# A four-layer mixer on one core: another fixed order of the same operations, and block 1's tiles turned by DMA

## The chip, the cores and the metric

The kernel runs on one core of a Trainium2 chip. Such a core has five engines that run side by side, each through its own list of instructions in order: TensorE (PE in the profile; its weight loads are PEld), VectorE (DVE), ScalarE (ACT), GpSimd (POOL) and SyncE (SP), which here only issues DMAs. The metric is the device time of one execution in microseconds (us), the median of several runs. Before the change it is 1176.29 us, the median of three runs from 1173.52 to 1176.73.

## The reference

The input x has 2048 positions of 512 features. Two kinds of layer alternate, A, B, A, B, each added to x, and both A layers share their weights, as do both B layers. LN is a layer norm without gain.

```python
# A: sliding attention, 32 heads of 16, 8 keys at distances 0, 2, .., 14 behind
q, k, v = LN(x) @ wqkv
attn = softmax(q . k[pos - 2*j] / 4, over j)
x = x + (sum_j attn_j * v[pos - 2*j]) @ wo
# B, on y = LN(x):
h  = gelu(LN(y) @ w1)                 # four groups of 128 features,
hs = [h0 by +1, h1 by -1, h2 by +2, h3 by -2 positions] @ w2
y1 = y + hs
x  = x + y1 + gelu(LN(y1) @ w3) @ w4  # w3: 512 x 1792
```

## The kernel before

**Numbers.** Most products must keep nearly f32 accuracy with f16 matmuls. Each operand is a high f16 part and a low f16 part (the rest), and three matmuls (high-high, high-low, low-high, the list HLS) stand for one product. A product with 512 inner features and 512 columns is so a group of 12 matmuls.

**Tiling.** The 2048 positions are four blocks of 512, a block is four tiles of 128 rows. With two layers of each kind there are eight block stages, n = 0 to 7: n = 0 to 3 are the blocks of the first A and B layer, n = 4 to 7 those of the second. Per stage there are five parts:
- `p1_stream(n)`: normalises each tile, turns it (features onto the partitions), multiplies by wqkv (three groups a tile) and stores q, k, v to memory (`kvq_d`). The turned tile lies in one of two places `xt`. Stage 0 does this in f32 out of `p1_quarters`.
- `p2(n)`: attention in four units of eight heads: loads `q` and `kv`, products and sums on VectorE, exponentials on ScalarE; the result is turned into `oT`.
- `p3(n)`: the o-projection (12 matmuls a tile with wo), adds x, normalises (`sq_dev`, `power`, `normed`), turns the normalised tile `f` into the place `nT`, and then w1 (four groups of 12 on the whole block) with its gelu into `h`.
- `p4(n)`: w2 on shifted columns of `h` (a group of 12 a tile), normalises and turns again.
- `p5(n)`: 14 chunks of the MLP, each an up group (12 matmuls with w3) and the down-projections (with w4, 3 matmuls a tile) into `acc`. Stage 0 has three tiles here and stage 7 five, since a block's last tile needs the next block's first rows.

**Turning a tile.** There are two ways. `turn_split` does it on TensorE: four transposes of 128x128 f32 by `ident` into PSUM (`mm`), ScalarE's copy of the high part, then either VectorE's subtraction for the low part or, with `minus=True`, a matmul with `minus_id` that subtracts the high part inside PSUM and a second copy by ScalarE. `turn_dma` makes high and low parts before the turn and turns both with one transposing DMA that SyncE issues:

```python
act(key, lambda: A.activation(hv(0), n.t, AF.Copy, scale=sc), ...)   # or VectorE
op(key, [(DVE, lambda: V.tensor_sub(hv(1), n.t, hv(0)), None),
         (POOL, lambda: G.tensor_sub(hv(1), n.t, hv(0)), None)], ...)
op(key, [(SP, lambda: Y.dma_start_transpose(out(), hl.t), None)], ...)
```

The tuple `BY_DMA` names, for the four places where tiles are turned (p1, p3, p4 and p2 in this order), the stages that use `turn_dma`; `MINUS` names those whose `turn_split` uses `minus_id`.

**The order.** The parts only record operations with what they read and write, and with the engines that can do each (`alts`). Nothing is decided at run time: `ORDER` is one list of numbers, 4 x operation + choice of engine, and the instructions are issued in that order, each engine keeping its own. `SLOTS` gives, for every buffer that is used for a while (`mm`, `acc`, `f32`, `g`, `w` and so on), the number of the place that it takes. `KEEP` puts so many filler matmuls ahead of an operation of TensorE: they multiply `ones` by itself (128x256) into a PSUM place that is about to be used. Another 38 (`WARM`) stand at the very start. Since an engine can't overtake within its list, an operation that waits holds everything behind it on that engine.

All operations are issued through one helper, so every instruction of the profile has line L307, and tile names tell them apart.

Of the kernel before, what the change touches and what calls it, by code (L numbers as in the profile page):

```python
# [219 lines left out]
124030101225127334105621120410122314206121117530134025203121225221116035301  # L220
"""

KEEP = {32: 26, 21: 8, 59: 12, 43: 12, 1040: 5, 1048: 16, 1062: 14}


class Buf:
# [67 lines left out]
def tile_mixer(ctx, tc, x_d, wqkv_d, wo_d, w1_d, w2_d, w3_d, w4_d, out_d):  # L294
# [351 lines left out]
    BY_DMA = (4, 5, 6, 7), (2, 3, 4, 5, 6, 7), (1, 2, 3, 4, 5, 6, 7), (2, 3, 4, 5, 6, 7)  # L646
# [712 lines left out]
```

## Time and profile before

| What | us |
|---|---|
| median of three runs | 1176.29 |
| the profiled execution's span | 1172.6 |
| TensorE busy in it | 1155.8 |
| VectorE busy | 895.6 |
| ScalarE busy | 630.4 |
| GpSimd busy | 453.3 |

The profiled execution has no time of its own beside its span: 1172.6 us from its first instruction to its last, 3.7 below the median of the runs. The granted TensorE clock is 1.000 of full speed in the mean over it. Busy times are the time in which at least one instruction of an engine is running; matmuls follow each other in a pipeline, so the time that one holds the engine is the difference of two starts and not its duration. DMA queues move 206.86 MB in all, and the 16 DMA engines are busy for some 61% of the span.

### The profile page before, as it was taken

To read this page: it belongs to the slowest core of one execution; us is meant where nothing else is said; L and a number is where in the kernel's file an instruction comes from. 1 tells how busy PE (TensorE), PEld (TensorE's weight loads), DVE (VectorE), ACT (ScalarE), POOL (GpSimd) and SP (SyncE) were. 2 spreads that over 40 slices of the span, in tenths; PEclk is the share of its full clock that TensorE was granted. 3 is DMA by queue.
4 is the path that set the end of the run, shared out by engine and by line. 5 is a ranking of instruction groups with operands and counts; after the bars stand their busy time and mean duration, and the time that the engine had idled before them with its cause. 6 is when DMAs were issued, how large, how long until landed. Compare 5 with 4: busy or idle time off the path is not lost.

```text
span 1172.6 us, 16187 instructions
## 1 busy us (share of the span) xinstructions
PE 1155.8 (99%) x5760; PEld 568.2 (48%) x5760; DVE 895.6 (76%) x1049; ACT 630.4 (54%) x1221; POOL 453.3 (39%) x441
## 2 busy tenths in 40 slices
PE   9999999899999999999999999999999999999998
PEld 7545555555444444444444444444444444444554
DVE  6888996999998996299976989999936999325112
ACT  5977667556656565464653446564534554444232
POOL 2746347226365455233432363632523272203000
PEclk9999999999999999999999999999999999999999
DMA  7687997365675646784567668873468366425221
GB/s 256 221 275 229 262 308 228 120 214 167 197 193 180 171 108 146 203 226 144 118 186 230 203 170 224 225 196 110 93 186 248 129 172 196 103 69 135 82 75 61
DMA packets 235161, 206.86 MB, mean 176 GB/s; under 512 B 107276, under 2 KB 160772, under 8 KB 235080
## 3 DMA queue, kind: packets, MB, share of 16 engines
q1 hardware_dynamic: 232796, 203.92, 60.5%
q10 hardware_dynamic: 2284, 1.91, 0.5%
q8 instruction: 45, 0.74, 0.3%
q14 instruction: 36, 0.29, 0.1%
HBM read 141.03 MB, written 39.47 MB: 154 GB/s over the span
## 4 chain that ended last, share of the span: by engine, by line
PE 79%; DMA 5%; DVE 4%; ACT 3%; issue 2%; POOL 1%; SPq 0%; ACTq 0%; POOLq 0%; DVEq 0%
PE mm L307 56%; PE acc L307 24%; DMA kvq_d<-ev 3%; DVE L L307 1%; DVE prod L307 1%; DMA xt<-g 1%; ACT junk L307 1%; DMA w<-in_B_w_dram 1%; DMA w<-in_A_x_dram 1%; ACT ev L307 0%; ACT f L307 0%; DVE f L307 0%; POOL g L307 0%; POOL f L307 0%; POOL a L307 0%
## 5 line engine op out<-in xcount | busy, mean ns | idle before, releaser
L307 POOL TENSOR_TENSOR g<-f,g 128x512 f16<-128x512 f32 (+1 forms) x122 | 187.9, 1550 | 315.9 <-ACT g L307 209.5
L307 PE MATMUL acc<-w,g 128*128 128x512 f16 x1302 | 298.3, 379 | 0.0
L307 PE MATMUL mm<-nT,w 128*128 128x512 f16 (+1 forms) x1344 | 292.7, 372 | 0.0
L307 ACT ACTIVATE mm<-mm,s_w 128x512 f32<-128x512 f32 (+2 forms) x158 | 98.4, 624 | 276.6 <-PE mm L307 275.8
L307 PEld LDWEIGHTS <-w 128*128 128x128 f16 x1512 | 141.7, 98 | 152.2
L307 PEld LDWEIGHTS <-g 128*128 128x128 f16 x1398 | 136.6, 98 | 157.6 <-issue 0.9
L307 PE MATMUL mm<-wq_hl,xt 128*128 128x512 f16 x864 | 194.0, 379 | 2.6 <-DMA xt<-g 1.5
L307 PEld LDWEIGHTS <-xt 128*128 128x128 f16 x1008 | 98.3, 98 | 120.1 <-DMA xt<-g 3.8
L307 DVE TENSOR_TENSOR prod<-kv,L 128x2048 f32<-128x2048 f32 (+1 forms) x44 | 146.7, 3336 | 0.1
L307 DVE TENSOR_REDUCE L<-prod 128x128 f32<-128x2048 f32 (+1 forms) x44 | 142.8, 3246 | 0.1
L307 DVE TENSOR_TENSOR prod<-kv,q 128x4096 f32<-128x4096 f32 (+1 forms) x38 | 132.3, 3482 | 7.9 <-DMA kv<-kvq_d 5.0
L307 DVE SCALAR_TENSOR_TENSOR g<-mm,c_g,g 128x512 f16<-128x512 f32 (+1 forms) x53 | 39.2, 740 | 89.8 <-ACT g L307 88.0
L307 DVE TENSOR_TENSOR prod<-prod 128x1024 f32<-128x1024 f32 (+2 forms) x56 | 89.7, 1605 | 0.1
L307 PE MATMUL mm<-nT,w_hl 128*128 128x512 f16 x384 | 87.4, 379 | 0.8 <-ACT nT L307 0.7
L307 PE MATMUL mm<-wo_hl,oT 128*128 128x512 f16 x384 | 86.5, 379 | 0.0
L307 PE MATMUL mm<-w_hl,h 128*128 128x512 f16 x384 | 85.7, 379 | 0.0
L307 ACT ACTIVATE g<-mm,c_g 128x512 f16<-128x512 f32 (+1 forms) x112 | 75.1, 672 | 1.9
L307 PEld LDWEIGHTS <-oT 128*128 128x128 f16 x426 | 41.5, 98 | 48.7 <-issue 0.2
L307 ACT ACT_TABLE_LOAD x42 | 53.9, 1283 | 11.5 <-DVE a L307 7.2
L307 PEld LDWEIGHTS <-w_hl 128*128 128x128 f16 x384 | 37.5, 98 | 45.8 <-issue 1.3
L307 PEld LDWEIGHTS <-h 128*128 128x128 f16 x384 | 37.5, 98 | 45.3 <-DVE h L307 0.4
L307 POOL COPY h<-h 128x2 f16<-128x2 f16 (+1 forms) x20 | 19.3, 982 | 76.2 <-DVE h L307 71.9
(227 smaller groups left out, 1361.7 us busy)
## 6 DMA issues: line engine op xcount, KB each, us to landing
w<-w SPq DMA_DIRECT2D x224, 256.0 KB, 2.7
kv<-kvq_d SPq DMA_DIRECT2D x62, 768.0 KB, 5.3
kvq_d<-ev SPq DMA_DIRECT2D x84, 256.0 KB, 3.0
w<-in_B_w_dram SPq DMA_DIRECT2D x28, 256.0 KB, 4.7
w<-g SPq DMA_DIRECT2D x28, 256.0 KB, 4.2
q<-kvq_d SPq DMA_DIRECT2D x28, 256.0 KB, 5.2
w<-in_A_x_dram SPq DMA_DIRECT2D x16, 256.0 KB, 6.0
x<-in_A_x_dram SPq DMA_DIRECT2D x16, 256.0 KB, 4.0
```

What stands on the lines that cost most here:

```text
L307: i = f(*a, **k).ins
```

## The change

Three lists and one tuple change. `BY_DMA` gets stage 1 in its second entry, so that the four tiles of `p3(1)` go through `turn_dma` rather than `turn_split` with `minus_id`. That replaces four operations a tile (transposes, copy, minus_id matmul, copy) by three (copy, subtraction, DMA); there are 3500 operations after, 3504 before. Each turned tile now takes a place `g` rather than a place `mm`. `ORDER` lists the operations in another order and with other engines for many of those that have a choice: the normalisations, the small operations of `power`, the copies out of PSUM, the two steps of `turn_dma`. `SLOTS` gives other places. `KEEP` goes from seven entries with 93 fillers to three with 70. The first TensorE tile of the list is now tile 0 rather than tile 1 of block 0, and the loads of its four x tiles stand at the head of SyncE's list.

```diff
 ORDER = [int(k) for k in """
-32 1756 20 16 12 8 24 1772 44 40 52 4 56 421 0 104 28 110 118 112 412 60 36 122 417 64 124 68 688 74 128 78 82 428 133
...
 SLOTS = """
-1002301101111010000011212230333200310100102012201301413021612123450331220120011400124255672325063144542571330132544327
...
+103200101000101030301022223111030021012110101201026450033450200126021100012010301000302710300414213503021001241322140
...
-KEEP = {32: 26, 21: 8, 59: 12, 43: 12, 1040: 5, 1048: 16, 1062: 14}
+KEEP = {21: 26, 32: 18, 1048: 26}
...
-    BY_DMA = (4, 5, 6, 7), (2, 3, 4, 5, 6, 7), (1, 2, 3, 4, 5, 6, 7), (2, 3, 4, 5, 6, 7)
+    BY_DMA = (4, 5, 6, 7), (1, 2, 3, 4, 5, 6, 7), (1, 2, 3, 4, 5, 6, 7), (2, 3, 4, 5, 6, 7)
```

In KEEP, 21, 32 and 43 are the turns of block 0's tiles 0, 1 and 2 at the start, 59 the first projection, 1040 the first w2 group of `p4(0)`, and 1048 and 1062 the first two turns behind it.

Read off the two lists, TensorE's order around block 1 is this. Before: the o-projections of block 1 lie among block 0's up and down groups, its four turns and minus_id matmuls among the last down-projections, and the last minus_id matmul stands directly ahead of the four w1 groups; then QKV of tile 1 of stage 4, with w2 of stage 1 between its groups, then of tiles 0 and 2. After: the last o-projection of block 1 is followed by three up and six down groups of block 0, then by the four w1 groups; then the three QKV groups of tile 1 of stage 4, four w2 groups, and QKV of tiles 2 and 0.

More of the change, by code (lines that the diff above doesn't have):

```diff
@@ L44 @@
 ORDER = [int(k) for k in """
[159 rows of a table removed]
[159 rows of a table added]
 """.split()]
 SLOTS = """
-1002301101111010000011212230333200310100102012201301413021612123450331220120011400124255672325063144542571330132544327
-4131031234405741343241130107521302413244265034115325017042333411454601512460012102130211133021201001331010020103103115
-1201302100210313000331302011110312100100033100210201111001300110033120112001111120050001111021330101130001100031330201
-1021100111001312011011011420211011101150120011110115101110211040211201100320311110321003102110033011611201013301020021
@@ L210 @@
-1003301042120101110114305783310103230113302123200041301001313231060505034374214132246031442044353571034022635122126042
-4330516351326130500203042233310213220043550142113471461032022352004410643725402141612217210542331326320145642017311450
-2311404203011314012001214201120311000011101011130110202010013100031210103301030002101110114175042561233213045102121044
-1025321114230410330122033060475163142023113061554115370561360201554331710136344051300002130430002151111000050600300002
-1011110115010210031100610011011101032102010330113328160510130153215210203143013540232514640613201235456017433432020630
@@ L215 @@
-5410526345513661031730210304431520014311400300041601100050101011051631003111210113100120010103110030101010331002300201
-1110114135070400042016353110135303040153206115253603210622371054221335206104520367502510035404303316222174353121255033
-1110041630212050630212110231313102110113101031020103101061001011331012212210011100204281043120031415630032534313226123
-0032402423210625241317322005246130123265435113324721203137314063102531516035224032031621601200115203345215601124323301
-2011557006214514160703223014510276043112256030216216122434172748122105515615510010211001333014153250320033512521300600
@@ L220 @@
-124030101225127334105621120410122314206121117530134025203121225221116035301
+103200101000101030301022223111030021012110101201026450033450200126021100012010301000302710300414213503021001241322140
+233132102103435120312002103451301332200125130112330020461210220011335671720600110011020111101101210010013122001001021
+310030010011201001001101102000100112101200000130011001000011101210000031210101110011300001012000000000111200111101210
+100000200000001401010110001001002101000010210111100000330100020012010011010001120110011031200020100001060101011000110
@@ new lines @@
+100201000010121010111001113760820000122403011002000100123123020007012311056221140302000036010740205100022106302147031
+150602300007140541321101105011112011201101032422153002042060123301017121200425415037060041037602120505411136030021207
+400016161240000111100110211001011000000010110000101001010201200110001101021010110115310201100010226057011112300411400
+102002201241402231034016012351203000711202403561000321710404625310606212150330204570004101000110200001001411101100002
+002120001010000100012001110011310210100001002102011100111313481301000010001113201051101252231004632120123603017040320
@@ new lines @@
+156064701032236100170325201241053004126221700251022020311022100200113000203101110100010100001050120011100112102101110
+011131000100001052206501400130360012030300200223211231044000601237101430121121502367360310407100411172151150262132350
+402000420130002100100000111110110000300001100101000010001200111101141021011000103210001011011131347111102212400521020
+035413106221010417025012310116210301327402121525006641103211700211433560023201041607028612200210041100010200120310442
+551123600101232110542230040760524000010365011430517100250103100670241010241350111102012104012010023141141055224630000
@@ L221 @@
+50310301230720110632101424115735106426117411102313104010101521113612107210120511234130116
 """
-KEEP = {32: 26, 21: 8, 59: 12, 43: 12, 1040: 5, 1048: 16, 1062: 14}
+KEEP = {21: 26, 32: 18, 1048: 26}
 class Buf:
```

317 rows, old and new, of the table ORDER are left out of this document.

## The prediction

> **What bounds the kernel now.** I read the head of the page first, for the engines' shares and the granted clock.
>
> ```profile
> span 1172.6 us, 16187 instructions
> PE 1155.8 (99%) x5760; PEld 568.2 (48%) x5760; DVE 895.6 (76%) x1049; ACT 630.4 (54%) x1221; POOL 453.3 (39%) x441
> PEclk9999999999999999999999999999999999999999
> ```
>
> TensorE is busy for 1155.8 of 1172.6 us at the full clock; no other engine is above 76%. Next, the busy time by stage, to see where the missing 16.8 us lie (columns: length, then busy us of PE, PEld, DVE, ACT, POOL).
>
> ```profile
> 0.00:50.00 50.00, 47.93 (x274) 34.88 (x275) 37.39 (x75) 35.22 (x87) 21.17 (x39) 1.00 0.69 224
> 200.00:250.00 50.00, 46.30 (x287) 28.92 (x286) 48.00 (x49) 29.92 (x60) 11.71 (x13) 1.00 0.46 156
> 340.00:440.00 100.00, 99.06 (x460) 44.75 (x459) 93.49 (x84) 58.64 (x95) 51.66 (x35) 1.00 0.60 162
> 540.00:640.00 100.00, 100.00 (x465) 45.31 (x464) 77.33 (x83) 48.22 (x92) 35.22 (x35) 1.00 0.61 170
> 1140.00:1173.00 33.00, 28.52 (x168) 14.21 (x166) 7.13 (x12) 6.70 (x14) 0.00 (x0) 1.00 0.18 63
> ```
>
> The stretch around 200 to 250 lacks 3.7 us, the first 50 us lack 2.1, 340 to 440 lacks 0.9, and the middle lacks nothing. The last row lacks 4.5, of which 0.4 lies beyond the end: there TensorE is done and only the last additions and stores remain. So about 12 us of idle time can be fought over; otherwise the end is the sum of TensorE's instructions, and VectorE is the one neighbour that is nearly as full (93 of 100 us) where attention runs. TensorE's own waits:
>
> ```profile
> PE mm L307 <- ACT nT L307: 2.6, 4, 1.0
> PE mm L307 <- DMA xt<-g: 1.5, 2, 0.9
> ```
>
> Each is at most 1 us. A change pays here only by taking instructions off TensorE or by closing such a wait, and costs only by opening one.
>
> **The change, part by part.** First the turns of block 1 behind the first attention. For each of four tiles TensorE now does four transposes and a matmul with minus_id, between down-projections (acc).
>
> ```profile
> 300.12 2.11 PE L307 MATMUL acc<-w,g 128*128 128x512 f16 x9
> 302.06 0.38 PE L307 MATMUL mm<-nT,minus_id 128*128 128x512 f16 x1
> 302.28 0.60 PE L307 MATMUL mm<-ident,f 128*128 128x128 f32 x4
> 302.71 2.11 PE L307 MATMUL acc<-w,g 128*128 128x512 f16 x9
> 304.65 0.38 PE L307 MATMUL mm<-nT,minus_id 128*128 128x512 f16 x1
> 305.72 10.52 PE L307 MATMUL mm<-nT,w_hl 128*128 128x512 f16 x48 [0.69 <-ACT nT L307]
> ```
>
> Durations overlap in the pipeline, so I take differences of starts: four transposes hold TensorE 0.43 us (302.28 to 302.71), the minus_id matmul 0.22 (302.06 to 302.28), nine matmuls 1.94 (300.12 to 302.06), so one is 0.216. Neither turned piece waits there, so all of it is on the path: 4 x 0.65 = **-2.6 us**. The wait of 0.69 before w1 (305.72) is for ScalarE's copy of the last turned tile; it goes too, but another arrival takes its place (below), so I count it nowhere.
>
> Second, the filler matmuls (on `ones`, for nothing but to keep TensorE running): KEEP falls from 93 in seven places to 70 in three; the 38 at the start stay.
>
> ```profile
> 1.04 9.83 PE L307 MATMUL mm<-ones 128*128 128x256 f16 x64 [1.04 <-DVE ones L307]
> 221.39 1.91 PE L307 MATMUL mm<-ones 128*128 128x256 f16 x16
> 221.84 0.77 POOL L307 TENSOR_SCALAR f<-f,c,c 128x512 f32<-128x512 f32 x1
> 223.14 0.60 PE L307 MATMUL mm<-ident,f 128*128 128x128 f32 x4
> ```
>
> One filler is (223.14 - 221.39) / 16 = 0.109 us, so 23 fewer are 2.5 us. But the fillers stand in for a wait: the tile that they precede is ready at 221.84 + 0.77 = 222.61 and TensorE takes it at 223.14, 0.53 late. If the waits stay, dropping four of the seven runs gives about 4 x 0.45 (a little under that 0.53, for the handover) = 1.8; if real work fills them, 2.5; if the waits grow, 0. I take **-1.8**, bounds 0 and -2.5. The new order does put more work there: in block 0's mixing, one run of 26 fillers, then three turns in a row, where the old order has 5, 16 and 14 in three places.
>
> Third, one wait that the order itself makes.
>
> ```profile
> 339.31 1.40 SPq L307 DMA_TRANSPOSE xt<-g  x1
> 343.25 4.06 PE L307 MATMUL mm<-wq_hl,xt 128*128 128x512 f16 x18 [0.94 <-DMA xt<-g]
> ```
>
> The second layer's QKV of block 0 takes tiles 1, 0, 2 through two xt places, and the old order finishes tile 1's last QKV group just two groups before tile 2's first. In the new order tile 1's three groups come together, then four w2 groups (4 x 12 x 0.216 = 10.4 us), then the next tile: its place is free long before. **-0.9**, bounds 0 and -0.9.
>
> Fourth, what arrives too late now. Tile 1 of that QKV comes right behind w1, and its input hangs on block 0's last down-projection, which starts at 302.71 above.
>
> ```profile
> 311.93 1.26 SPq L307 DMA_TRANSPOSE xt<-g  x1
> 316.23 0.76 PEld L307 LDWEIGHTS <-xt 128*128 128x128 f16 x5 [0.49 <-DMA xt<-g]
> 316.24 1.04 PE L307 MATMUL mm<-wq_hl,xt 128*128 128x512 f16 x4
> ```
>
> The weight load waits for the landing and gets it just in time: 13.5 us from the start of that down-projection. In the old order 1.94 + 0.22 (and the 0.69 of waiting and its handover) stand ahead of the 48 matmuls of w1; in the new one w1 follows at once, so TensorE comes after 1.94 + 10.37 = 12.3 us. The same chain is then late by **+1.2**, bounds 0 (VectorE gets to it sooner) and +3 (a further 1.8 us if an attention product stands ahead of it on VectorE).
>
> Fifth, the turned tiles themselves. Each now takes a scaled copy (ScalarE or VectorE), a subtraction (VectorE three times, GpSimd once) and one transposing DMA on SP. Block 7 already does this; its last tile is the quick case:
>
> ```profile
> 1015.23 2.75 PE L307 MATMUL mm<-wo_hl,oT 128*128 128x512 f16 x12
> 1018.02 0.75 DVE L307 SCALAR_TENSOR_TENSOR x<-mm,s_wo,x 128x512 f32<-128x512 f32 x1 [0.68 <-PE mm L307]
> 1024.28 1.23 SPq L307 DMA_TRANSPOSE nT<-g  x1
> nT<-g SPq DMA_TRANSPOSE x52, 4.2
> ```
>
> From the end of the o-projection (about 1017.8) to issue is 6.5 us and to landing 4.2 more (the median of the last row), 10.7 in all. The new order has nine block 0 groups of 1.94 us (9 x 0.216 for a down-projection, the same for a three-tile up) between block 1's last o-projection and its w1: 17.5 us. So 0 is taken; the upper bound comes with the rivals. SP gets eight DMAs more: these four, two kv shifts of the start and two stores of the end, both from ScalarE's queue; behind each stand the weight and kv loads.
>
> ```profile
> SPq L307 <- PE mm L307: 219.7, 99, 9.2
> ```
>
> SP spends 219.7 us waiting for TensorE to free places, so 4 x 1.23 us of issuing is covered; without that cover it would be 4.9 us on the loads. The shifts come while TensorE still has its first projections. Both end stores are issued while TensorE still runs (bounds 0 and +0.5).
>
> Sixth, places and engines. Counted over the two lists, TensorE goes from 541 to 533 operations, ScalarE 1028 to 1006, VectorE 894 to 880, GpSimd 390 to 422, SP 651 to 659. Off TensorE these cost nothing in themselves: TensorE's work is what hides them. Attention keeps its distance: between the last QKV group and the first o-projection of block 7 lie 111.5 us of TensorE work in both orders, and 114.1 for block 5.
>
> Sum: -2.6 - 1.8 - 0.9 + 1.2 = -4.1 us on the profiled execution, 1172.6 to 1168.5. That execution's span lies 3.7 below the median 1176.29; I carry the 3.7 over: **1172.2 us**.
>
> **The rivals.** Where two results of this kernel differ by under 0.3% (3.5 us) they can't be told apart.
>
> *The gain is eaten.* The fillers' 2.5 us come back as plain waits (in the first 25 us the tiles depend on loads and on ScalarE, which the list doesn't speed up), the xt wait moves elsewhere, and two new waits of 1 us open. For it: every wait above is 1 us or less, so the old list was already tight. Against it: the 2.6 us of turns are sure. -2.6 + 1.2 + 1 = -0.4: about 1175.9.
>
> *Slower: block 1's tiles arrive late at w1.* The nine groups run while VectorE does the attention of block 2, as when block 2's own tiles were turned:
>
> ```profile
> 392.47 2.75 PE L307 MATMUL mm<-wo_hl,oT 128*128 128x512 f16 x12
> 416.35 2.60 SPq L307 DMA_TRANSPOSE nT<-g  x2
> 417.35 4.41 DVE L307 TENSOR_TENSOR prod<-kv,L 128x4096 f32<-128x4096 f32 x1
> 418.08 4.70 POOL L307 TENSOR_TENSOR g<-f,g 128x512 f16<-128x512 f32 x1 [2.20 <-ACT g L307]
> 423.55 0.81 PE L307 MATMUL mm<-nT,w_hl 128*128 128x512 f16 x3
> ```
>
> From the end of that o-projection (395.06) to issue are 21.3 us, and 4.2 to land: 25.5. If block 1's last tile took as long, w1 would wait 25.5 - 17.5 = 8.0 us, and the QKV behind it would still pay its 1.2 to 3: -2.6 - 1.8 - 0.9 + 8.0 + 3 = +5.7, 1182. It decides from 4.1 us of lateness at w1, where the sum turns positive. Against it: part of the 21.3 us was the old list's choice, since w1 came only at 423.55. For it: GpSimd's subtraction of a 128x512 tile took 4.70 us next to VectorE's product of 4.41, and this alone:
>
> ```profile
> 1014.70 1.16 POOL L307 TENSOR_TENSOR g<-f,g 128x512 f16<-128x512 f32 x1 [1.91 <-ACT g L307]
> ```
>
> The new list gives GpSimd 32 more operations, nine of them such subtractions. [...]
>
> *More is won.* The 26 fillers with three turns behind them really close the hole at 200 to 250 (3.7 us idle plus 30 fillers, 3.3 us), and the late QKV isn't late: -2.6 - 2.5 - 0.9 - 3.7 = -9.7, 1166.6. Against it: the mixing's chain of small operations between w2 and the turns stays as it is.
>
> That the edit does nothing is no rival: the eight operations are gone from TensorE's list.
>
> **How the numbers follow.** Forecast 0.45, eaten 0.25, slower 0.18, more won 0.12. The forecast's own spread is 1169.5 to 1174.5. For the range I go down to 1165, a little below the rival of more gain, and up to 1180, which takes in the eaten gain and half of the late tiles. Faster by over 0.3% means under 1172.8: a good 0.38 of the forecast's 0.45 and all 0.12 make 0.50. The same: 0.07 and 0.23 of the eaten gain, 0.30. Slower by over 0.3%, above 1179.8: part of the late tiles, and a little for an opening that I don't see, 0.20.
>
> **What would show it.** Right: in block 1 behind the attention no transposes of f on TensorE, `nT<-g` 56 times rather than 52 on SP, 20 fewer matmuls and 23 fewer fillers (5717 in all); TensorE's idle time no more than 1 or 2 us above 16.8; a wait of about 1 us for xt at the first second-layer QKV, and none where 343.25 stands now. Wrong: a wait of several us for `nT<-g` before w1 of block 1 (late tiles), an idle share above 20 us with waits on ScalarE before 250 us (eaten), or GpSimd's subtractions well above their present mean beside VectorE's products with something of TensorE's behind them.

## The result, and the profile after

The changed kernel takes 1182.41 us (median of four, 1179.96 to 1185.08) against 1175.01 for the kernel before: a ratio of 1.0064, 95% interval 1.0042 to 1.0086. Timed again beside other kernels it stood at 1.0069 (1.0054 to 1.0084). So it is 7 to 8 us slower, outside the forecast range of 1165 to 1180 and on the other side of no change.

The profiled execution of after has a span of 1178.2 us, 5.6 above that of before. The head of its page:

```profile
span 1178.2 us, 16138 instructions
PE 1150.2 (98%) x5717; PEld 563.5 (48%) x5717; DVE 896.8 (76%) x1033; ACT 631.6 (54%) x1207; POOL 491.4 (42%) x473
```

TensorE has 5717 matmuls, as forecast, and 5.6 us less work (1155.8 before). But it idles 28.0 us rather than 16.8: +11.2. The busy time by stage shows where (columns as before: length, then busy us of PE, PEld, DVE, ACT, POOL, then granted clock). First after, then the three rows of before that the prediction doesn't show.

```profile
0.00:50.00 50.00, 44.66 (x250) 31.82 (x251) 31.90 (x63) 35.42 (x85) 18.14 (x38) 1.00 0.67 221
50.00:100.00 50.00, 45.78 (x255) 25.23 (x253) 41.65 (x61) 39.32 (x84) 37.38 (x32) 1.00 0.83 264
100.00:150.00 50.00, 47.02 (x258) 26.25 (x259) 42.83 (x44) 29.45 (x59) 20.15 (x16) 1.00 0.82 242
200.00:250.00 50.00, 48.99 (x298) 30.16 (x297) 45.52 (x46) 31.86 (x60) 16.25 (x17) 1.00 0.55 174
300.00:340.00 40.00, 33.77 (x155) 14.98 (x156) 34.65 (x52) 24.25 (x51) 19.98 (x25) 1.00 0.76 189
```

```profile
50.00:100.00 50.00, 47.24 (x261) 25.59 (x260) 42.17 (x53) 40.60 (x91) 29.11 (x26) 1.00 0.87 271
100.00:150.00 50.00, 49.85 (x273) 27.70 (x272) 45.58 (x42) 30.00 (x61) 24.02 (x21) 1.00 0.88 256
300.00:340.00 40.00, 39.31 (x185) 17.83 (x184) 38.38 (x50) 25.33 (x55) 22.39 (x23) 1.00 0.65 177
```

Length less PE busy is the idle time of a stage. The first 150 us idle 12.5 us (5.34 + 4.22 + 2.98) where before idled 5.0: +7.6. The stage around 300 idles 6.2 rather than 0.7: +5.5. The hole at 200 to 250 did shrink, from 3.7 to 1.0, and 340 to 440 lost its 0.9 (TensorE is busy for 99.94 us there). Between 740 and 840 after idles 1.7 us where before idles nothing, in one wait of 1.73 us for VectorE; no experiment looks at it. TensorE's waits in after, grouped:

```profile
PE mm L307 <- ACT f L307: 4.2, 5, 1.0
PE acc L307 <- POOL g L307: 4.2, 2, 2.2
...
PE mm L307 <- DMA xt<-g: 2.3, 1, 2.3
PE mm L307 <- ACT x L307: 2.0, 1, 2.0
```

Before had no wait over 1.1 us; after has four of 1.9 to 2.3. The same point in both traces gives the lag of after along the way (the start of the instruction; for the last matmul, its end):

| TensorE reaches | before | after | lag |
|---|---|---|---|
| first turn behind block 0's w2 | 223.14 | 227.82 | +4.7 |
| block 0's last down-projection | 302.71 | 303.56 | +0.9 |
| block 1's w1 | 305.72 | 307.61 | +1.9 |
| first QKV of the second layer | 316.24 | 320.40 | +4.2 |
| last matmul | 1168.52 | 1173.86 | +5.3 |

How far can one pair of traces be trusted? Eight traces of kernels that share after's list up to that first turn (after, its repetition a1, and p1 to p4, q1 and t1 below) reach it between 226.83 and 231.68 us; six that share before's list up to there (before, m1, s1, s3 to s5) between 223.14 and 226.41. So the new head, the part of the list up to this turn, is slower by some 5 us, but a single trace is good to a few us only.

**The stage around 300.** The timeline of after, rows of the engines in order of time:

```profile
289.21 0.20 POOL L307 TENSOR_SCALAR b<-b 128x4 f32<-128x4 f32 x1
290.75 2.28 DVE L307 TENSOR_TENSOR prod<-kv,L 128x2048 f32<-128x2048 f32 x1
290.88 2.25 POOL L307 TENSOR_SCALAR b<-b 128x4 f32<-128x4 f32 x1
293.11 2.54 POOL L307 TENSOR_SCALAR b<-b,b 128x1 f32<-128x1 f32 x1
293.28 2.29 DVE L307 TENSOR_TENSOR prod<-kv,q 128x2048 f32<-128x2048 f32 x1
295.62 0.91 POOL L307 TENSOR_TENSOR g<-f,g 128x384 f16<-128x384 f32 x1
295.69 0.82 ACT L307 ACTIVATE f<-x,b,b 128x512 f32<-128x512 f32 x1 [4.32 <-POOL b L307]
302.04 2.12 PE L307 MATMUL acc<-w,g 128*128 128x512 f16 x9 [2.24 <-POOL g L307]
303.51 2.53 POOL L307 TENSOR_TENSOR g<-f,g 128x384 f16<-128x384 f32 x1 [1.52 <-ACT g L307]
306.09 1.68 PE L307 MATMUL acc<-w,g 128*128 128x512 f16 x7 [1.94 <-POOL g L307]
313.54 1.43 POOL L307 TENSOR_TENSOR g<-f,g 128x512 f16<-128x512 f32 x1
316.45 1.28 SPq L307 DMA_TRANSPOSE xt<-g  x1
320.40 2.98 PE L307 MATMUL mm<-wq_hl,xt 128*128 128x512 f16 x13 [2.26 <-DMA xt<-g]
```

GpSimd's list has the small operations of block 1's norm ahead of block 0's low parts (`g<-f,g`). Two of them, of 4 and of 1 number a partition, take 2.25 and 2.54 us: each ends just after VectorE's product beside it does (293.13 and 293.03, 295.65 and 295.57). One of the same form as the first took 0.20 us at 289.21, beside a reduction of VectorE. ScalarE waits 4.32 us for the second, to normalise tile 3, and its gelu for chunk 12 is queued behind. So the low parts of the last chunks come late, and two down-projections wait 4.2 us in all. There is no wait for `nT` before w1.

**The clock.** The profiled execution of after has the full clock throughout (1.00 in every row above), but most others don't. Its ten executions have mean granted clocks of 0.996 to 1.000, 0.997 in the mean; the 21 of before timed beside the second six have 0.999 or 1.000. The difference of about 0.0024 is an estimated 2.8 us of 1180. What happens is seen by comparing after (first fence) with the kernel of the experiment t1 below (second and third: timeline, then windows), which is the same up to there:

```profile
59.35 0.38 PE L307 MATMUL mm<-ss_w,ones 128*128 128x1 f32 x2 [1.97 <-ACT x L307]
59.60 2.11 PE L307 MATMUL acc<-wq_hl,g 128*128 128x384 f16 x12
```

```profile
59.08 0.38 PE L307 MATMUL mm<-ss_w,ones 128*128 128x1 f32 x2 [1.73 <-ACT x L307]
59.33 3.79 PE L307 MATMUL acc<-wq_hl,g 128*128 128x384 f16 x12
```

```profile
59.00:60.00 1.00, 0.92 (x5) 0.59 (x6) 1.00 (x2) 0.64 (x2) 1.00 (x1) 0.78 0.91 260
60.00:61.00 1.00, 1.00 (x4) 0.45 (x3) 1.00 (x1) 0.81 (x2) 0.74 (x1) 0.50 0.65 194
62.00:63.00 1.00, 1.00 (x6) 0.54 (x5) 1.00 (x1) 1.00 (x3) 0.81 (x1) 0.52 1.06 300
```

The same wait comes in both. In one execution the twelve matmuls behind it take 2.11 us, in the other 3.79, at a clock of 0.50 from about 59.6 to 63.0. Such a stretch of some 3.4 us costs 1.7 us. In six traces of the experiments that lost clock (p1, p2, s1, s2, t1, k0), every stretch at 0.50 ahead of the last matmul began within some 2 us of the end of a wait of TensorE of 1.4 to 3.9 us, though not every such wait is followed by one.

### The profile page after: what moved, and what is told of

The parts are those of the page before. It is cut to its first block, busy times and chain, and to the rows that moved or that the text cites. A ratio compares the mean times of both kernels' runs of the same rounds, so it can differ in the third digit from the quotient of the medians.

```text
span 1178.2 us, 16138 instructions
## 1 busy us (share of the span) xinstructions
PE 1150.2 (98%) x5717; PEld 563.5 (48%) x5717; DVE 896.8 (76%) x1033; ACT 631.6 (54%) x1207; POOL 491.4 (42%) x473
## 5 line engine op out<-in xcount | busy, mean ns | idle before, releaser
L307 POOL TENSOR_TENSOR g<-f,g 128x512 f16<-128x512 f32 (+1 forms) x131 | 223.4, 1717 | 257.3 <-ACT g L307 166.6
L307 DVE TENSOR_TENSOR prod<-kv,L 128x2048 f32<-128x2048 f32 (+1 forms) x44 | 149.3, 3395 | 1.4 <-PE mm L307 1.2
L307 POOL TENSOR_TENSOR b<-b,nhalf 128x1 f32<-128x1 f32 (+1 forms) x40 | 44.5, 1113 | 30.3 <-ACT b L307 15.0
```

The costliest lines, as they stand in the source:

```text
L307: i = f(*a, **k).ins
```

## The experiments

Numbers of `ORDER` are 4 x operation + choice; a row of a diff is an entry of that list.

**GpSimd's list.** p1 changes the engine of one operation, the product at 293.11 above.

```diff
 ORDER = [int(k) for k in """
...
-4949
+4948
...
```

> After, with one choice of engine changed: the last small product of block 1's norm (tile 3, 128x1) is on ScalarE, as before, instead of behind GpSimd's four small operations, where it ran from 293.11 to 295.65 and held the normalised tile, ScalarE's next gelu, and GpSimd's low part of chunk 11. Theory 'GpSimd's list' (TensorE's waits of 2.24 and 1.94 us before the down-projections at 302.04 and 306.09 hang on that chain): both fall under 0.5 us and the kernel is 3 to 4 us faster than after, 1178 to 1179, ratio 1.003. [...]

Measured: 1179.40 us, ratio 1.0038 (1.0024 to 1.0053). The last three down-projections, 27 matmuls, follow each other without a wait, so the 4.2 us are gone, and the ratio lies below after's second interval. But the QKV behind then waits 3.85 us. The timeline of p1:

```profile
300.93 5.99 PE L307 MATMUL acc<-w,g 128*128 128x512 f16 x27
321.33 1.89 PE L307 MATMUL mm<-wq_hl,xt 128*128 128x512 f16 x4 [3.85 <-ACT h L307]
```

The view puts that wait down to ScalarE's `h`; but the DMA of xt went out at 317.54, 3.8 us ahead of the QKV, much as in after (316.45 and 320.40), so xt is the likelier cause, and p2 below tests it. q1 leaves the product on GpSimd and moves only the four small operations (4968, operation `powers`) behind the last low part.

```diff
-4968
...
 4752
+4968
```

> After with one operation moved: GpSimd's four small operations (128x4) of block 1's norm of the sum, 289.21 to 293.12 there, go behind the low part of block 0's last chunk. Nothing else changes; the product 128x1 that ran behind them stays on GpSimd. Theory 'the four small operations hold GpSimd's list': the product runs by 290, the low part of chunk 11 by 293, the waits of 2.24 and 1.94 us before the down-projections are under 0.5 us, 3 us faster than after, ratio 1.003 to 1.0045 (as with the product on ScalarE, 1.0038). Rival 'the product and what else stands in the list': the waits stay, ratio 1.006 to 1.007.

Measured: 1178.73 us, 1.0033 (1.0021 to 1.0045). The timeline of q1:

```profile
290.64 0.30 POOL L307 TENSOR_SCALAR b<-b,b 128x1 f32<-128x1 f32 x1
298.66 5.99 PE L307 MATMUL acc<-w,g 128*128 128x512 f16 x27
305.42 10.53 PE L307 MATMUL mm<-nT,w_hl 128*128 128x512 f16 x48 [0.77 <-DMA nT<-g]
317.40 5.79 PE L307 MATMUL mm<-wq_hl,xt 128*128 128x512 f16 x26 [1.45 <-DMA xt<-g]
```

The product takes 0.30 rather than 2.54 us, and 27 matmuls of three down-projections run in 5.99 us. Another account of after's waits, that the subtractions are late wherever they stand, falls: what stood ahead of them made them late. From the first turn behind w2 to block 1's w1, after takes 79.8 us in both of its traces, p1 75.5 and q1 76.2.

**SyncE's list.** p2 takes p1 and exchanges two DMAs on SyncE.

```diff
-6324
...
 5868
+6324
```

> The kernel with the one product on ScalarE (1179.4 us, ratio 1.0038), and one exchange on SyncE: the transposing DMA of xt for the first second-layer QKV goes ahead of the load of x that stood before it. In that kernel xt's low part was ready at 314.49, but SyncE, held by the load of x, issued the DMA only at 317.54; the QKV began at 321.33 after 3.85 us without work, and TensorE's clock was 0.50 for some 3.4 us right behind. Theory 'SyncE's list' (the load waits for a place that the stores of x at 309.93 free): the DMA goes out by 315, the wait for xt falls under 1 us, no reduced clock there; 2 to 3 us faster, 1176.5 to 1177.5, ratio 1.002. Rival 'landing' (the transposing DMA is slow to land among the others whatever its place): the wait stays at 2 us or more, ratio 1.003 to 1.004.

Measured: 1175.43 us, 1.0010 (1.0001 to 1.0020), 4.0 us less than p1 by the medians, 3.3 by the ratios, and a little more than expected. The two edits together take the ratio from 1.0064 or 1.0069 to 1.0010: two entries of the list held 6 to 7 of the 7 to 8 us that after had lost. In the profiled execution, though, the wait for xt was still 2.2 us, so the first theory is right on the list and wrong on the wait. The timeline of SyncE in p1, then in p2:

```profile
316.86 0.59 SPq L307 DMA_DIRECT2D x<-in_A_x_dram  x1
317.54 1.27 SPq L307 DMA_TRANSPOSE xt<-g  x1
```

```profile
309.45 3.10 SPq L307 DMA_TRANSPOSE oT<-g  x1
313.22 2.93 SPq L307 DMA_TRANSPOSE xt<-g  x1
```

Now the DMA is issued when its data are ready, but issuing takes 2.93 us. p3 therefore puts xt's DMA ahead of that of block 2's oT.

```diff
-3128
...
 5868
+3128
```

> The kernel with the product on ScalarE and xt ahead of the load of x (1175.43 us, ratio 1.0010), and the transposing DMA of block 2's oT (issued at 309.45 for 3.10 us) behind that of xt instead of ahead of it. There xt's DMA was ready at 313.19 and took 2.93 us to issue rather than 1.27; the QKV began at 318.22 after a wait of some 2.2 us, with the clock lowered behind it. Theory 'transposing DMAs queue up' (the second is held while the first is in progress): xt issues in 1.3 us, the wait falls to about 1 us and the clock stays: 1 to 2.5 us faster, ratio 0.999 to 1.000. Rival 'VectorE, GpSimd or the other queues slow the issue': the wait stays at 2 us or more, ratio 1.001.

Measured: 1175.76 us, 1.0009 (0.9998 to 1.0019). The timeline of p3:

```profile
309.88 1.24 SPq L307 DMA_TRANSPOSE xt<-g  x1
302.69 10.31 PE L307 MATMUL mm<-nT,w_hl 128*128 128x512 f16 x47
313.13 7.94 PE L307 MATMUL mm<-wq_hl,xt 128*128 128x512 f16 x36
```

Here the QKV follows w1 without a wait, yet the median is no lower than p2's. The place in SyncE's list is what held xt; that the wait had still cost p2's median anything is not shown, and so it stays open how p2's edit gained its 3 to 4 us.

**The turns.** t1 is after's list with block 1 turned on TensorE again, m1 is before's list with block 1 turned by DMA; besides the line shown, the operations of the turn change in `ORDER` and their places in `SLOTS`.

```diff
-    BY_DMA = (4, 5, 6, 7), (1, 2, 3, 4, 5, 6, 7), (1, 2, 3, 4, 5, 6, 7), (2, 3, 4, 5, 6, 7)
+    BY_DMA = (4, 5, 6, 7), (2, 3, 4, 5, 6, 7), (1, 2, 3, 4, 5, 6, 7), (2, 3, 4, 5, 6, 7)
```

> After, with block 1's four tiles turned on TensorE as before (16 transposes and 4 products with minus_id, 2.6 us of TensorE) at the places in the list where the copies, subtractions and DMAs of the turn stand now. Theory 'the edit is worth its 2.6 us' (TensorE's work is the time): 1182.4 + 2.6 = 1185.0, ratio 1.0085. Rival 'the turns covered other work' (block 0's late low parts, 4.2 us of waits, and QKV's wait of 2.3 us for xt stand right behind the place that the turns left, so the 2.6 us are only waited for elsewhere, and GpSimd and ScalarE have less to do): 1180 to 1182.5, ratio 1.005 to 1.006, with the wait for xt gone.

Measured: 1183.11 us, 1.0073 (1.0056 to 1.0089). Against after's 1.0064 and 1.0069 that is 0.5 to 1 us more, with intervals that overlap so far that neither 0 nor 2.6 is excluded. The traces say more. From the first turn behind w2 to block 1's w1 after takes 79.8 us twice (227.82 to 307.61, and 231.37 to 311.18 in a1), t1 82.0 (231.68 to 313.71), none of them with a lowered clock on the way. The 2.2 us between them are most of the 2.6: the first theory is nearer for that stretch. The turns do cover most of the two waits before the down-projections (0.4 us in place of 4.2, though two new waits of 0.4 and 1.1 us open), but not the wait for xt, which is still some 2 us.

> Before's order, engines and fillers, with the edit alone: block 1's four tiles turned by DMA. The twelve operations of the turn stand in the list right behind the normalised tile 0 (291.29 before; the four turned tiles are written in the order 0 to 3), the copy on ScalarE, the subtraction on VectorE three times and on GpSimd once, as after has them. Theory 'the edit is worth its TensorE time, less the late xt' (w1 follows the last down-projection 2.6 us earlier, and the chain of 13.5 us to the second-layer QKV, just in time before, is then late by 1.2 to 2.3): -0.3 to -1.4 us, ratio 0.9985 to 1.0000, no wait for nT<-g. Rival 'late tiles' (four transposing DMAs from 293 on, one after another, and 4 us to land): w1 waits 1 to 5 us for nT<-g, ratio 1.001 to 1.004.

Measured: 1184.66 us, 1.0086 (1.0073 to 1.0100): 10 us slower than before, worse than both cases. The timeline of m1:

```profile
298.16 0.63 ACT L307 ACTIVATE g<-f 128x512 f16<-128x512 f32 x1 [3.54 <-DMA nT<-g]
302.28 3.00 POOL L307 TENSOR_TENSOR g<-f,g 128x384 f16<-128x384 f32 x1 [5.55 <-ACT f L307]
305.34 2.27 PE L307 MATMUL acc<-w,g 128*128 128x512 f16 x7 [2.95 <-POOL g L307]
325.44 5.74 PE L307 MATMUL mm<-wq_hl,xt 128*128 128x512 f16 x15 [6.38 <-DMA xt<-g]
```

The tiles do not arrive late at w1. But each turn holds a place `g` until its DMA has landed. The third copy waits 3.54 us for such a place, ScalarE's gelu of chunk 13 is queued behind it, the last low part and down-projection are late, VectorE reaches the sum at 313.82 (303.56 before) and the QKV waits 6.38 us. Behind these two waits of TensorE the clock is at 0.50 for 10.2 us in all; TensorE is busy for 8 of them, which costs an estimated 4 us more. The edit needs room in the list that the old order does not have; the placing in m1 is mine, and a better one may cost less.

**The fillers and the clock.** k0 takes all fillers but the first 38 out of before.

```diff
-KEEP = {32: 26, 21: 8, 59: 12, 43: 12, 1040: 5, 1048: 16, 1062: 14}
+KEEP = {}
```

> Before, without its 93 fillers (10.1 us of TensorE work for nothing); the 38 at the start stay. Theory 'waits lower the clock': the fillers stood in waits, which now are plain waits of up to 3 us; mean clocks fall to 0.994 to 0.998, and the kernel is 0 to 5 us slower than before, ratio 1.000 to 1.004, although the 10.1 us of work are gone. Rival, the price of the prediction's second step (dropping fillers is worth a little under 0.45 us a run of them, seven runs): 3 us faster, ratio 0.997, at a mean clock of 1.000.

Measured: 1179.93 us, 1.0044 (1.0032 to 1.0056), mean clocks 0.994 to 0.996 in all five: 5.0 us slower with 10.1 us less work. Where the last two runs of fillers were, TensorE now waits, and the clock falls to 0.50 there, which it does nowhere in before's profiled execution. A window of k0, as above:

```profile
228.00:232.00 4.00, 2.73 (x11) 2.08 (x12) 4.00 (x7) 2.92 (x7) 0.49 (x1) 0.50 0.01 2
```

The same happens at 11 to 18 us, behind a wait of 3.19 us where the first fillers were. In the two stretches TensorE is busy for 9.8 us at 0.50, so an estimated 4.9 us are lost. The span of k0's profiled execution is 1176.5 us, 3.9 above before's. Without the lowered clock it would be some 1 us below: dropping the fillers does save a little, as the rival says, and the clock takes more than that back. f1 goes the other way and puts 78 fillers into the waits of p2.

```diff
-KEEP = {21: 26, 32: 18, 1048: 26}
+KEEP = {21: 26, 32: 18, 1048: 34, 215: 16, 270: 8, 694: 8, 722: 10, 841: 8, 855: 12, 1474: 8}
```

> The kernel of the run with xt ahead, with 78 fillers more (8.5 us of TensorE work for nothing), put ahead of TensorE's waits of the first 165 us (16 before the sum for w2 at 59.35, 8 at 72.9, 8 at 99.9, 10 at 122.0, 8 at 146.35, 12 at 158.27), before the first turn behind w2 (34 rather than 26) and before the first second-layer QKV (8). Theory 'waits lower the clock' (behind waits of some 1.5 to 4 us the granted clock is 0.50 for about 3.4 us, 1.7 us lost each, in some executions of one kernel and not in others): every run has a mean clock of 0.999 or 1.000, the runs lie closer together, and the median is no higher than without the fillers or up to 2 us lower. Rival 'a filler costs its 0.11 us' (the clock has nothing to do with it): mean clocks from 0.996 to 1.000 as before, and 1 to 4 us slower where the fillers overrun the waits.

Measured: 1181.05 us, 1.0057 (1.0038 to 1.0076), 5.6 slower than p2, clocks of 0.998 in five of six. So these fillers cost more than they save and did not keep the clock up everywhere: the theory as put fails here. Its traced execution is the one at 1.000; what lowers the clock in the others stays open. The repetition of after has the same limit:

> After itself once more, beside the others, for its spread. Theory 'waits lower the clock': executions with a mean clock of 1.000 lie at 1178 to 1181 us, and 0.001 less of it (0.7 of a stretch of 3.4 us at half clock) costs 1.2 us more, so that 0.996 is at 1183 to 1185.5; the median is 1181 to 1183, ratio 1.0055 to 1.0075, with over half of the executions under 1.000. Rival: times that don't follow the clock.

Measured: 1183.59 us, all six executions under 1.000, but two of them, at 0.996 and 0.997, took 1180.6 us. The clock accounts for part of the time and not for its spread.

**The engines.** g1 keeps after's order and gives each operation the engine of before (425 entries).

> After's order, with the engine of before for every operation that both have: 419 operations go to another engine of VectorE, ScalarE and GpSimd (64 net leave GpSimd or come to it: 128 leave it, 97 come) and 6 DMAs to the other queue. Theory 'engines' (step 6's zero was wrong because of where the small operations run): the waits at 302, 306 and 320 go, ratio 1.000 to 1.003. Rival 'order' (the position in each engine's list decides, and the engines were chosen to fit it): the waits stay or new ones open, ratio 1.006 or more.

Measured: 1222.05 us, 1.0398 (1.0378 to 1.0418). The engines of one order don't fit the other: engine and place in the list can't be priced apart, and the counts of operations by engine that the prediction compared don't price either.

**The head.** s1 is before's list up to the first turn behind block 0's w2 (883 entries) and after's from there; s2 the mirror of it (893 entries of after's).

> The list of before up to the first turn behind block 0's w2 (TensorE reaches it at 223.14 us before, at 227.82 after), then the list of after; fillers and engines go with their part. What changed has a lag of +4.7 us at that point, +0.8 a little later (227.82 against 223.14, then 232.36 against 231.59), and +5.6 at the end. Theory 'places add up' (each stretch has its own losses and gains, and nothing later takes up an early lag): 1182.4 - 4.7 = 1177.7 us, a ratio to before of 1.002 to 1.003. Rival 'handed on' (the mixing behind w2 waits for VectorE's attention or for loads, so it takes up what the head lost, which is why the lag falls to 0.8 there): no change against after, 1181.5 to 1182.5, ratio 1.006.

> The mirror of it: the list of after up to the first turn behind block 0's w2, then the list of before, with block 1 turned on TensorE as before. 'Places add up': 1175.0 + 4.7 = 1179.7 us, ratio 1.004. 'Handed on': 1175 to 1176, ratio 1.000 to 1.001, with the lag of the head gone behind the mixing.

Measured: s1 1184.51 us, 1.0091 (1.0071 to 1.0111); s2 1180.51 us, 1.0048 (1.0033 to 1.0063). In before's list the new head costs 5.6 us, about its lag. But the old head in after's list gains nothing (s1's interval overlaps both of after's). s1 reaches the turns 3.5 us sooner than after and waits there for ScalarE; with a clock of 0.50 from 301.5 it is level with after at the last down-projection (303.82 against 303.56), and 0.9 us ahead at w1. The timeline of s1 (its list takes one line less, hence L306):

```profile
224.36 0.60 PE L306 MATMUL mm<-ident,f 128*128 128x128 f32 x4
227.05 0.66 PE L306 MATMUL mm<-ident,f 128*128 128x128 f32 x4 [2.09 <-ACT f L306]
```

s3 is s1 with p2's two edits, s4 is s3 with block 6's four small operations on GpSimd behind that block's low parts.

> Before's list up to the first turn behind block 0's w2, then the list with the product on ScalarE and xt ahead of the load of x. With the old head and after's own rest TensorE reached the last w2 group 3.75 us sooner than in after, but stood 2.26 us before the second turn waiting for ScalarE's f, and was level with after at the last down-projection of block 0 (303.82 against 303.56). Theory 'handed on' (the head's time is taken back by the mixing's chain of small operations and by block 1's attention on VectorE): no more than 1 us against 1175.4, ratio 1.000 to 1.001. Rival 'places add up, once GpSimd's list is mended': 4 to 5 us faster, 1170.5 to 1171.5, ratio 0.9965.

> The kernel with the old head, the product on ScalarE and xt ahead of the load of x (1179.76 us, ratio 1.0039), and one operation moved: GpSimd's four small operations of block 6's norm go behind that block's low parts. Theory 'GpSimd's list again': the wait of 3.67 us before block 6's w1 falls under 1 us, with no lowered clock behind it, and what the head saved is kept to the end: 1172.5 to 1174.5, ratio 0.998 to 1.000. Rival 'handed on': VectorE's attention or a load holds the next stage instead, 1178 to 1180, ratio 1.003 to 1.004.

Measured: s3 1179.76 us, 1.0039 (1.0024 to 1.0055), worse than p2 with its later head; s4 1177.13 us, 1.0027 (1.0013 to 1.0040). In their traces s3's lead over p2 is 3.2 us before block 6, of which 1.7 are a stretch of lowered clock that p2 has more, and is lost at block 6's w1. The timeline of s3, then that of s4:

```profile
891.44 5.16 POOL L307 TENSOR_TENSOR b<-b,nhalf 128x4 f32<-128x4 f32 x1
918.83 4.44 PE L307 MATMUL mm<-nT,w_hl 128*128 128x512 f16 x12 [3.50 <-DMA nT<-g]
```

```profile
914.46 2.75 PE L307 MATMUL mm<-nT,w_hl 128*128 128x512 f16 x12 [1.39 <-DMA nT<-g]
```

Moving GpSimd's operations takes 2.1 us off the wait, the way its theory has it, though 1.39 us are left and not under 1. The time fell by 2.6 us, with intervals that overlap, and lies between what the theory and the rival expected. Last, the mended kernel (p3, with the small operations of blocks 1 and 6 moved) with the new head, p4, and with the old one, s5.

> After mended, with its own head: the product on ScalarE, xt ahead of the load of x and of oT, and GpSimd's four small operations of blocks 1 and 6 behind the low parts. No wait stood before block 6's w1 in the kernel without the last two moves (1175.76 us, ratio 1.0009), so they free little: 1174.5 to 1175.8, ratio 1.000 to 1.001.

> The same mended kernel with before's list up to the first turn behind block 0's w2. Theory 'places add up once the GpSimd lists are mended': the 3.2 us that the old head still had at 770 us stay, 3 us below p4, 1171.5 to 1172.5, ratio 0.9975 to 0.9985, faster than before. Rival 'handed on': within 1 us of p4.

Measured: p4 1177.18 us, 1.0022 (1.0011 to 1.0032); s5 1177.22 us, 1.0021 (1.0011 to 1.0031). p4 misses its expectation: the further moves gained nothing. s5 is where "handed on" puts it. In its trace s5 is 6.4 us ahead of p4 at the first turn (223.56 against 230.01) and 0.2 at block 1's w1, for which it waits:

```profile
305.23 12.22 PE L307 MATMUL mm<-nT,w_hl 128*128 128x512 f16 x48 [2.37 <-DMA nT<-g]
```

The lead goes in three pieces: 2.10 us of waiting for ScalarE at the second turn, 1.7 of half clock behind that (from 227.98), and these 2.37. The other traces, for the same stretch (s1 and s3 to s5 each have 1.7 us of loss by half clock in it, the others none):

| kernel | first turn behind w2 | block 1's w1 | between |
|---|---|---|---|
| before | 223.14 | 305.72 | 82.6 |
| after and a1 | 227.82, 231.37 | 307.61, 311.18 | 79.8, 79.8 |
| p1 to p4, new head | 226.83 to 231.49 | 302.46 to 306.96 | 75.3 to 75.6 |
| s1, old head | 224.36 | 306.74 | 82.4 |
| s3, s4, s5, old head | 226.41, 223.54, 223.56 | 305.08, 304.17, 305.23 | 78.7, 80.6, 81.7 |

With the product off GpSimd (p1 to p4) the stretch is 4 us shorter than in after, and the old head gives back most of its lead in it. No kernel tried beats before: p2 and p3 come to within 0.1%.

## Why the prediction was wrong

Its sum was -4.1 us on the profiled execution; it measured +5.6, and an estimated 2.8 us more in the mean of its executions through the clock. The 3.7 us that it carried over from span to median were too many as well: in every execution timed here the time is 1.7 to 1.9 us above the span.

- **Block 1's turns, -2.6: right as work, and nearly as time.** TensorE's busy time fell by 5.6 us, close to the 5.1 of the turns (2.6) and the 23 fillers (2.5). In this order they are worth 2.2 us up to w1 (t1's trace); what is left of it at the end, 0.5 to 1 us in the medians, is within the noise.
- **Fillers, -1.8: not borne out.** They were costed as a stand-in for a wait, with no loss possible. k0 shows 5.0 us lost when before gives up all of its own. The term left out is the clock behind a plain wait (0.50 from 228 to 232 us in k0); the profile showed a clock of 1.00 everywhere, and I took that as given rather than as what the fillers kept. The new head has +4.7 us of lag although it has run 9 fillers fewer by the first turn (70 against 79). That is "the gain is eaten" by its place, waits on ScalarE before 250 us and 28.0 us of idle time, the signs that the prediction gave for it. But that rival spoke of two waits of 1 us and its sum counted only one. What in the new head costs its 5 us, the fillers or the order of loads and tiles, no run takes apart.
- **The wait at 343.25, -0.9: right.** 340 to 440 idles 0.06 us.
- **The late QKV, +1.2: right in direction and within its bounds.** The wait is 2.26 us, where the sum had 1.2. The chain of 13.5 us was taken over from before; in after it takes 16.8 (303.56 to 320.40): 1.9 us are that down-projection's own wait for its low part, and 1.5 pass between the low part of xt (ready at 314.97) and its DMA (316.45), behind a load on SyncE. The step looked at neither.
- **The turned tiles, 0: right.** No wait for `nT` in after. It appears once the waits ahead of w1 are gone: 0.77 us in q1, 1.45 in s4, 2.4 in s5.
- **Places and engines, 0: this step failed.** "TensorE's work is what hides them" held for their sum and not for their place in a list. Two small operations on GpSimd cost TensorE 4.2 us (p1, q1). The same holds of "4 x 1.23 us of issuing is covered" on SyncE: the waits there are long in sum, but the one DMA of xt stood behind a load, and moving it brought 3 to 4 us (p2). The size of the first cost could be read in before's own trace, where the same small product stands beside VectorE's sum `prod<-prod` (373.12 to 375.41, 2.29 us) and takes 2.48 us:

```profile
373.01 2.48 POOL L307 TENSOR_SCALAR b<-b,b 128x1 f32<-128x1 f32 x1
```

- **The rival "late tiles at w1", 1182** met the time by chance. Its mechanism, GpSimd stretched beside VectorE's products, is the one that the runs show (2.25 and 2.54 us in after beside products, 0.20 in after and 0.30 in q1 beside reductions); its place was block 0's last chunks and not w1, and the stretched operations were those of 1 and 4 numbers, which the prediction did not cost at all. The tiles' own subtractions grew too, from 1.56 to 1.73 us in the mean (128x512), the third sign that it gave.

Whether the head's lag is added to the rest depends on the list behind it, and the prediction lacked this step. In before's list it was added (s2). In after's it was not (s1, s5): between 220 and 305 us the mixing's small operations (w2 and the norm behind it) and block 1's chain from attention to `nT` are the next to be late, so most of the time won earlier turns into waits there, and into half clock behind them.

## What to carry to other kernels

Where every engine works through a list, look not at how much an engine has to do but at what stands directly ahead of the operation that TensorE waits for, on each engine and on the DMA queue. Time won on TensorE is kept only where the next operand is early; beside a late operand it turns into a wait: of s5's 6.4 us of lead on p4, 0.2 were left at block 1's w1. A clock at full speed in the profile can hang on small waits, and a wait can be paid for twice: before, with no wait over 1.1 us in its trace, had mean clocks of 0.999 or 1.000, and k0, timed beside it without the fillers, 0.994 to 0.996; in t1 a wait of 1.73 us had 3.4 us at half clock behind it, which cost another 1.7.

## What was not expected of the hardware

- GpSimd's smallest operations took about as long as a whole product of VectorE: the one on 128x1 takes 0.30 us beside a reduction (q1, 290.64) and 2.54 beside a product of 2.29 (after, 293.11); `b<-b,nhalf` on 128x4 takes 1.02 us in after (289.49) and 5.16 in s3 (891.44), beside a product of 4.43. The ends lie close together: in after, 290.88 + 2.25 = 293.13, and the product ends at 293.03. What stretches them no run shows.
- A wait of 1.73 us was followed by 3.4 us at half clock in t1. In p1 and p2 such a stretch (at 75 and at 73 us) came behind waits of 1.4 us at most, and in after the clock stayed at 1.00 behind one of 2.24. What decides between the two no run shows.
- Issuing a transposing DMA took 1.24 us in p3 and 2.93 in p2, where another that had taken 3.10 stood ahead. In p3 the two followed each other at 1.24 and 1.29, so that one stands ahead is not reason enough; the cause stays open.
